# The first attention of an attention and GELU kernel: a shift added in PSUM, a new order of its steps, and two small loads that change queues

## The chip, the cores and the metric

The kernel runs on one core of one Trainium2 chip. Its time is the device time of one execution in microseconds (us). All times inside an execution count from the start of the profiled span.

## What is computed

q and k ([8, 12, 448, 64]: batch, head, position, dimension) are normalised by their root mean square and scaled by a gain; then follow softmax attention with v, and two dense layers with a GELU between them. The reference, cut to that:

```python
def rmsnorm(x, g):
    rms = np.sqrt(np.mean(x * x, axis=-1, keepdims=True) + 1e-06)
    return x / rms * g
q_n, k_n = (rmsnorm(q, g_q), rmsnorm(k, g_k))
scores = q_n @ k_n.transpose(0, 1, 3, 2) / 8.0
attn = softmax(scores)                  # max taken off, exp, divided by the sum
x = (attn @ v).transpose(0, 2, 1, 3).reshape(3584, 768)
h = x @ w_in                            # 768 -> 2048
c = np.float32(np.sqrt(2.0 / np.pi))
g = 0.5 * h * (1.0 + np.tanh(c * (h + 0.044715 * h * h * h)))
return g @ w_out                        # 2048 -> 768
```

In place of each row's maximum the kernel takes one shift for all scores off the exponent, worked out from the gains: `shift = min(0, 60 - bound)`, where the bound comes from the largest product of the two gains (L824 to L837). It does not change the quotient.

## The kernel before

**Tiling.** A batch has three groups (c = 0, 1, 2) of four heads. In a group, q and k lie on 128 partitions as 2 heads x 64 rows, with two pairs of heads (a) and seven pieces (t) of 64 positions beside each other. A unit (L327) is the scores of one piece of k against all 448 positions of q, for four heads: four matmuls of 64x64 weights, which fill a PSUM tile `t` of 128 x 2 x 448. There are two such tiles in the first attention, taken in turn (`pair`, L70). `exp` (L338) is one ScalarE instruction per unit: exp(scale x scores + shift), 128x896, written in bf16. So a batch has 21 units and 21 exponentials.

**What a group needs before its units.** The raw loads; squares (`square`, L157) and their sums along a row (`total`, L170, on VectorE); `rsqrt` (L193): a Ln and one or two Exp on ScalarE that give 1/root-mean-square; `normed` (L271): raw times that root, in bf16; `turn` (L289): transposes on TensorE, 128x128 each, seven for q and seven for k, into a PSUM bank `tp`; `put` (L299): the copy out of it into `qT` and `kT`, on VectorE for most, where k is also multiplied by both gains. k is normed and turned in two parts, pieces 0 to 3 (`t_first`) and 4 to 6 (`t_rest`).

**What follows the units.** `products` (L369): the sums of the exponentials (weights `ones`) and their products with v, in packs of four matmuls; then on VectorE a transpose of the sums (`turned`, L391), the reciprocal, its spread over the partitions (`spread`, L402) and the multiplication into `xT` (`quad_x`, L416). The first layer (`mm1_pair`, L541) reads `xT` and `w_in`; the second reads `w_out` and is laid between the units of the next batch's attention (L488, the quartered matmuls).

**What sets the order.** The program is scheduled by hand: each engine does its instructions in the order in which the code issues them. The first attention (L700) goes through slots 0 to 20: the loads of `side`, one unit, its exponential, then the steps that `mid` (L852) lists for the slot. Ahead of it stand the loads, the norms of group 0 and the shift. Idle matmuls (`idle`, L266) fill TensorE there. The bank pool `ps_m` has two PSUM banks; the transposes, the roots of group 2 and the sums of groups 1 and 2 share them.

**Queues.** q and k are asked for by SyncE's queue (SP), except the second half of the very first q, which ScalarE's queue asks for, followed there by g_k. v, w_in and w_out go through GpSimd's queue (POOL), in POOL's program order, between the squares that POOL does.

Of the kernel before, what the change touches and what calls it, by code (L numbers as in the profile page):

```python
# [17 lines left out]
def kernel(  # L18
# [20 lines left out]
    R = 64  # L39
# [48 lines left out]
    def load_g(i, row, eng):  # L88
        eng.dma_start(
            grow[:, i].rearrange("(j p) d -> j p d", j=2)[:, 0],  # L90
            row.rearrange("(j d) -> j d", j=2),
        )
# [12 lines left out]
    shift = consts.tile([P, 1], F32)  # L105
    eps = consts.tile([P, 1], F32)
    win = wts.tile([128, HP, d_ff], BF16)
# [62 lines left out]
    def total(b, c, n, hs=both, ts=slice(0, NT)):  # L170
        if b not in sss:
            sss[b] = smp.tile([P, NCH, 2, 2, NT], F32, tag="ss", name="ss")
        nc.vector.reduce_sum(  # L173
            sss[b][:, seat(b, c), "qk".index(n), hs, ts], squares(b, c, n, hs, ts), axis=AX.X
        )
# [17 lines left out]
    def rsqrt(b, c=slice(0, NCH), ns=both, near=(), ts=slice(0, NT), twice=False):  # L193

        if b not in rinvs:
            rinvs[b] = smp.tile([P, NCH, 2, 2, NT], F32, tag="rinv", name="rinv")
        lg = smp.tile([P, NCH, 2, 2, NT], F32, tag="lg", name="lg")
        nc.scalar.activation(  # L198
            lg[:, c, ns, :, ts], sss[b][:, c, ns, :, ts], AF.Ln, scale=1.0 / D, bias=eps
        )  # L200
# [124 lines left out]
    exs, ess, oas, scs = {}, {}, {}, {}  # L325

    def unit(b, c, t):  # L327

        sc = scs[b, c, t] = pair("sc")
        for a in range(2):  # L330
            rs = slice(a * D, (a + 1) * D)
            for r in range(2):
                nc.tensor.matmul(  # L333
                    sc[r * R:(r + 1) * R, a, :S], kT[rs, c, t, r], qT[b][rs, c, :, r],
                    start=True, stop=True,
                )

    def exp(b, c, t):  # L338
        if (b, c) not in exs:
            exs[b, c] = exq.tile([P, NT, 2, S], BF16, tag="ex", name="ex")  # L340
        nc.scalar.activation(  # L341
            exs[b, c][:, t], scs.pop((b, c, t))[:, :, :S], AF.Exp, scale=scale, bias=shift
        )
# [383 lines left out]
    def plan(*entries):  # L727
        steps = {}
        for slot, *fns in entries:
# [7 lines left out]
    halves += [  # L737
        lambda ts=ts: nc.sync.dma_start(  # L738
            raws["k", 0, 0][:, :, ts].rearrange("p a t d -> p a (t d)"),
            k[0, :4].rearrange("(a r) (p t) d -> r p a t d", r=2, t=NT)[:, :, :, ts]  # L740
            .rearrange("r p a t d -> (r p) a (t d)"),
        )
        for ts in (t_first, t_rest)
    ]
# [7 lines left out]
    nc.vector.memset(eps, 1e-6)  # L752
    for i in range(3):
        nc.vector.memset(ones[:, i * D // 4:(i + 1 + i // 2) * D // 4], 1.0)
    for i in range(2):
        nc.vector.memset(rows[:, i * P // 2:(i + 1) * P // 2], (D ** 0.5) * (1 + 2.0 ** -7))

# [52 lines left out]
    normed(0, 0, "q", nc.gpsimd, t_first)  # L810
    normed(0, 0, "q", nc.vector, t_rest)
    normed(0, 0, "k", nc.vector, t_first)
    total(0, 0, "k", ts=t_rest)
    square(0, 1, "q", nc.gpsimd)
    for a in range(2):
        square(0, 1, "k", nc.gpsimd, slice(a, a + 1))
    load_v(0, 0, 2)
# [3 lines left out]
    w_in_part(0, 2)  # L821
    for j in range(2):
        rs = slice(j * 32, (j + 1) * 32)
        nc.tensor.matmul(gall[:, j, :32], rows[rs], gbf[rs], start=True, stop=True)  # L824
    for ts in (t_rest, t_first):
# [7 lines left out]
    put(0, 0, "k", slice(0, 1))  # L833
    nc.vector.tensor_reduce(
        shift, gall[:, :, :32], axis=AX.XY, op=ALU.max, apply_absolute_value=True, negate=True
    )
# [5 lines left out]
    for a in range(2):  # L842
        total(0, 1, "k", slice(a, a + 1))

# [7 lines left out]
    mid = [(0, lambda: idle(2, warm())),  # L852
           (1, lambda: turn_new(0, t_rest), lambda: idle(2, warm())),
           (2, lambda: rsqrt(0, 1, near=(0, 1)), lambda: idle(2, warm())),
           (3, lambda: put(0, 0, "k", t_rest), lambda: normed(0, 1, "q", nc.vector),
            lambda: normed(0, 1, "k", nc.vector, t_first), lambda: idle(2, warm())),
           (4, lambda: idle(2, warm())),
           (5, lambda: turn(0, 1, "q"), lambda: put(0, 1, "q"),
            lambda: turn_new(1, t_first), lambda: put(0, 1, "k", t_first)),
           (6, lambda: total(0, 2, "q"), lambda: total(0, 2, "k")),  # L860
           (7, lambda: products(0, 0, 0, 0, 3)),
# [9 lines left out]
           (9, lambda: turn(0, 1, "k", t_rest), lambda: put(0, 1, "k", t_rest),  # L871
            lambda: normed(0, 2, "k", nc.vector, t_first),
            lambda: normed(0, 2, "k", nc.vector, t_rest), lambda: recip()),
           (10, lambda: products(0, 0, 1, 0, 3)),

           (11, lambda: products(0, 0, 1, 3, 5), lambda: turn(0, 2, "k", t_first),
            lambda: put(0, 2, "k", t_first), lambda: spread(slice(0, 1))),
           (12, lambda: turn(0, 2, "q"), lambda: put(0, 2, "q")),
           (13, lambda: turn_new(2, t_rest), lambda: put(0, 2, "k", t_rest),
# [156 lines left out]
```

## Time and profile before

| | us |
|---|---|
| median of 3 runs | 392.43 |
| lowest and highest | 391.71, 393.4 |
| the profiled execution | 392.21 |
| its span | 390.4 |
| PE (TensorE) busy | 381.5 (98%) |
| ACT (ScalarE) busy | 278.7 (71%) |
| DVE (VectorE) busy | 238.0 (61%) |
| POOL (GpSimd) busy | 125.2 (32%) |

The granted TensorE clock was 1.00. In the rows, `start us, us, engine line op out<-in shape xcount [idle before <-who ended it]` stands for one instruction or a run of equal ones; PEld is TensorE's weight load, an engine with a q behind it is its sequencer, which issues transfers. A row of the chain of waits has start, duration and what the end waited for in that time. A row of the windows has the stretch, its length, the busy time of each engine with the count of its instructions, the granted clock, the share of the 16 transfer engines and GB/s. A row of the transfers ends with the time from issue to landing. Neighbouring instructions on ACT and DVE overlap by about 0.1 us in these rows, so a run of three is shorter than three times one.

### The profile page before, as it was taken

Reading aid. Unit: us, or ns where it says so; the run is one execution under the profiler, and the core shown is the slowest. Engines: PE = TensorE matmul, PEld = TensorE weight load, DVE = VectorE, ACT = ScalarE, POOL = GpSimd, SP = SyncE. Lnnn points to the kernel's source line nnn. Section 1 sums busy time; section 2 is a strip of 40 time slices with the busy share of each in tenths; the row PEclk is TensorE's granted clock in tenths of the full one; section 3 lists DMA queues with packets and bytes.
Section 4 is the critical chain, followed back from the end, with each engine's and each line's share of the span. In section 5 each row is a group of like instructions: output and inputs, shape, how many; then the busy total and the mean of one; then the engine's idle time right before and its main releaser. Section 6 shows DMA issues by size and latency. Waiting matters only on the chain.

```text
span 390.4 us, 17468 instructions
## 1 busy us (share of the span) xinstructions
PE 381.5 (98%) x8023; PEld 290.2 (74%) x8023; DVE 238.0 (61%) x367; ACT 278.7 (71%) x353; POOL 125.2 (32%) x107
## 2 busy tenths in 40 slices
PE   8799999999999999999999999999999999999996
PEld 3365567777888788877888778877888778887664
DVE  5899938976597258835689256963598304980010
ACT  6895589767994689747996589946897449944300
POOL 4996504485004540083302740064400900000000
PEclk9999999999999999999999999999999999999999
DMA  8999999999713993359932996159622831220033
GB/s 272 311 212 210 210 169 330 210 210 240 150 44 87 230 217 73 80 104 234 194 78 65 157 273 113 44 111 249 107 64 64 123 44 35 52 65 4 2 81 82
DMA packets 64414, 54.68 MB, mean 140 GB/s; under 512 B 37588, under 2 KB 59988, under 8 KB 64340
## 3 DMA queue, kind: packets, MB, share of 16 engines
q1 hardware_dynamic: 53904, 41.33, 45.7%
q0 software_dynamic: 10128, 11.80, 18.5%
q8 instruction: 63, 1.03, 1.1%
q10 hardware_dynamic: 308, 0.43, 0.3%
q14 instruction: 11, 0.09, 0.1%
HBM read 45.61 MB, written 11.01 MB: 145 GB/s over the span
## 4 chain that ended last, share of the span: by engine, by line
PE 92%; ACT 4%; DMA 2%; POOL 1%; SPq 0%; DVE 0%; issue 0%; DVEq 0%
PE t L530 33%; PE t L488 32%; PE t L385 9%; PE t L333 7%; PE t L461 5%; PE t L549 4%; ACT ex L341 4%; DMA rawq<-in_q_dram 2%; POOL g L164 1%; PE h L434 1%; PE tp L294 0%; PE o L385 0%; SPq L738 0%; PE os L385 0%; DVE ss L173 0%; ACT lg L198 0%
## 5 line engine op out<-in xcount | busy, mean ns | idle before, releaser
L341 ACT ACTIVATE ex<-t,shift 128x896 bf16<-128x896 f32 x168 | 156.1, 1013 | 1.8 <-PE t L333 1.6
L488 PE MATMUL t<-wout,g 64*64 64x384 bf16 (+1 forms) x3456 | 151.5, 305 | 0.0
L530 PE MATMUL t<-xT,win 64*64 64x448 bf16 x2688 | 128.6, 349 | 0.0
L488 PEld LDWEIGHTS <-g 64*64 64x64 bf16 x3456 | 112.7, 107 | 20.6 <-issue 0.6
L530 PEld LDWEIGHTS <-win 64*64 64x64 bf16 x2688 | 96.4, 107 | 30.8
L536 ACT ACTIVATE g<-t 128x896 bf16<-128x896 f32 x56 | 50.5, 914 | 57.2 <-PE t L530 57.2
L173 DVE TENSOR_REDUCE ss<-sq 128x14 f32<-128x896 f32 (+3 forms) x45 | 44.6, 997 | 52.8 <-ACT sq L162 48.9
L333 PE MATMUL t<-qT,kT 64*64 64x448 bf16 x672 | 58.6, 351 | 3.1 <-ACT lg L198 1.6
L353 DVE TENSOR_TENSOR es<-ex 128x1792 bf16<-128x1792 bf16 x20 | 21.2, 1058 | 32.1 <-ACT ex L341 32.1
L276 POOL TENSOR_TENSOR nrmq<-rawq,rinv 128x896 bf16<-128x896 f32 (+1 forms) x21 | 34.7, 1652 | 16.5 <-ACT rinv L205 9.9
L786 POOL COPY mark<-es 1x1 bf16<-1x1 bf16 x6 | 1.1, 176 | 116.8 <-DVE es L360 112.6
L276 POOL TENSOR_TENSOR nrmk<-rawk,rinv 128x896 bf16<-128x896 f32 x20 | 33.7, 1686 | 0.0
L333 PEld LDWEIGHTS <-kT 64*64 64x64 bf16 x672 | 25.4, 106 | 10.4 <-DVE kT L303 3.6
L385 PE MATMUL t<-ex,vb 64*64 64x448 bf16 x588 | 32.1, 350 | 0.0
L395 DVE STREAM_TRANSPOSE st<-t 128x448 f32<-128x448 f32 x42 | 24.8, 627 | 9.3 <-PE t L385 9.3
L385 PEld LDWEIGHTS <-vb 64*64 64x64 bf16 x672 | 23.6, 107 | 7.0 <-issue 0.8
L407 DVE STREAM_TRANSPOSE rb<-rc 128x896 f32<-128x896 f32 (+1 forms) x25 | 26.7, 1067 | 0.3
L694 DVE COPY osb<-t 128x384 f32<-128x384 f32 (+1 forms) x4 | 2.0, 508 | 35.2 <-PE t L461 35.2
L420 DVE TENSOR_TENSOR xT<-t,rb 128x896 bf16<-128x896 f32 x21 | 22.8, 1087 | 0.8
L164 POOL TENSOR_TENSOR sq<-rawq 128x896 f32<-128x896 f32 (+1 forms) x9 | 13.6, 1515 | 28.3 <-DVE ss L173 21.6
L506 ACT COPY osb<-t 128x768 f32<-128x768 f32 (+1 forms) x18 | 12.6, 701 | 14.0 <-PE t L488 14.0
L356 DVE TENSOR_TENSOR es<-es,ex 128x1792 bf16<-128x1792 bf16 x20 | 21.3, 1063 | 0.8 <-ACT ex L341 0.8
(103 smaller groups left out, 313.6 us busy)
## 6 DMA issues: line engine op xcount, KB each, us to landing
rawq<-in_q_dram SPq DMA_DIRECT2D x23, 448.0 KB, 5.1
rawk<-in_k_dram SPq DMA_DIRECT2D x23, 448.0 KB, 6.0
out_dram<-osb SPq DMA_DIRECT2D x42, 192.0 KB, 2.7
vb<-in_v_dram POOLq DMA_DIRECT2D x6, 672.0 KB, 7.0
win<-in_moe_w_in_dram POOLq DMA_DIRECT2D x8, 384.0 KB, 11.1
wout<-in_moe_w_out_dram POOLq DMA_DIRECT2D x3, 768.0 KB, 18.4
out_dram<-osb SPq DMA_DIRECT2D x24, 96.0 KB, 3.1
vb<-in_v_dram POOLq DMA_DIRECT2D x2, 448.0 KB, 15.4
```

Source lines behind the costliest of these rows:

```text
L173: nc.vector.reduce_sum(sss[b][:, seat(b, c), "qk".index(n), hs, ts], squares(b, c, n, hs, ts), axis=AX.X)
L276: eng.tensor_mul(nrms[n, b, c][:, ts].rearrange("p t a d -> p a t d"), raws[n, b, c][:, :, ts], root[:, :, ts].to_broadcast([P, 2, m, D]),)
L333: nc.tensor.matmul(sc[r * R:(r + 1) * R, a, :S], kT[rs, c, t, r], qT[b][rs, c, :, r], start=True, stop=True,)
L341: nc.scalar.activation(exs[b, c][:, t], scs.pop((b, c, t))[:, :, :S], AF.Exp, scale=scale, bias=shift)
L356: nc.vector.tensor_add(es, es, ex[:, 4:6])
L385: nc.tensor.matmul(o[r][a * D:(a + 1) * D], vb[b % 2][rs, 2 * c + a, i] if what else ones[rs], es[i][rs, a], start=(i == 0), stop=(i == n ...
L395: nc.vector.transpose(st[:, r].rearrange("p a b -> p (a b)"), o[r])
L407: nc.vector.transpose(oas["rb"][:, rs].rearrange("p r s -> p (r s)"), rc.to_broadcast([128, (rs.stop - rs.start) * m, 32]),)
L420: nc.vector.tensor_mul(xT[b][:, 2 * c:2 * c + 2], oas["o", c, 1][:, :, :S], oas["rb"])
L488: mm = nc.tensor.matmul(o[a * R:(a + 1) * R, bank, :hi - lo], g[rs, f, at:at + R], wout[rs, f, lo:hi], start=(turn == 0 and f == 0), stop= ...
L530: mm = nc.tensor.matmul(h[a * R:(a + 1) * R, j, :S], win[rs, c, at:at + R], xT[b][rs, c], start=begin and c == cs[0], stop=end and c == cs ...
L536: nc.scalar.activation(g[:, 2 * i:2 * i + 2, (b % 2) * S:(b % 2 + 1) * S], h[:, :, :S], AF.Gelu_apprx_tanh,)
```

## The change

It touches the start and the first attention alone.

1. For units 2 to 13 the shift is added to the scores in PSUM: four more matmuls ahead of the unit's own, with weights `shifts` (the shift in bf16, 64 columns) and a moving tile `eighth` of 0.125, which open the accumulation that the scores close. The exponential of these units has the constant 0 as its bias. The others still read the tile `shift`. The Ln of every `rsqrt` has a constant 1e-6 as bias, not the tile `eps`.
2. The second half of the square of k of group 1 moves from POOL to ScalarE, behind exponential 1, and its sum to that slot.
3. `mid` is written anew: the copy of the rest of k of group 0 moves from slot 3 to 2, the transposes and copies of group 1 from slot 5 to 6, the norm of the rest of k of group 2 from slot 9 to 12, the reciprocal and the first half of its spread from 9 and 11 to 12. Ten idle matmuls become six.
4. The shift is worked out earlier on DVE; the rest of the first k is asked for by ScalarE's queue, and g_k by SyncE's behind the first k.

```diff
+    def in_psum(b, c, t):
+        return b == 0 and 2 <= c * NT + t < 2 * NT
+
     def unit(b, c, t):
         sc = scs[b, c, t] = pair("sc")
-        for a in range(2):
+        parts = [(a, r) for a in range(2) for r in range(2)]
+        begun = in_psum(b, c, t)
+        if begun:
+            for a, r in parts:
+                rs = slice(a * D, (a + 1) * D)
+                nc.tensor.matmul(
+                    sc[r * R:(r + 1) * R, a, :S], shifts[rs], eighth[rs], start=True, stop=False
+                )
...
-                    start=True, stop=True,
+                start=not begun, stop=True,
...
-            exs[b, c][:, t], scs.pop((b, c, t))[:, :, :S], AF.Exp, scale=scale, bias=shift
+            exs[b, c][:, t], scs.pop((b, c, t))[:, :, :S], AF.Exp, scale=scale,
+            bias=0.0 if in_psum(b, c, t) else shift
...
-            lg[:, c, ns, :, ts], sss[b][:, c, ns, :, ts], AF.Ln, scale=1.0 / D, bias=eps
+            lg[:, c, ns, :, ts], sss[b][:, c, ns, :, ts], AF.Ln, scale=1.0 / D, bias=1e-6
...
-        for ts in (t_first, t_rest)
+        for ts, eng in ((t_first, nc.sync), (t_rest, nc.scalar))
...
-    load_g(1, g_k, nc.scalar)
+    load_g(1, g_k, nc.sync)
...
-    nc.vector.tensor_scalar(shift, shift, 60.0, 0.0, op0=ALU.add, op1=ALU.min)
+    nc.vector.tensor_scalar(
+        shifts, shift.to_broadcast([P, R]), 60.0, 0.0, op0=ALU.add, op1=ALU.min
+    )
+    nc.vector.tensor_copy(shift, shifts[:, :1])
...
+           (1, lambda: square(0, 1, "k", nc.scalar, slice(1, 2)),
+            lambda: total(0, 1, "k", slice(1, 2)),
...
-           (5, lambda: turn(0, 1, "q"), lambda: put(0, 1, "q"),
+           (6, lambda: turn(0, 1, "q"), lambda: put(0, 1, "q"),
...
+           (12, lambda: turn(0, 2, "q"), lambda: put(0, 2, "q"),
+            lambda: normed(0, 2, "k", nc.vector, t_rest), lambda: recip(),
+            lambda: spread(slice(0, 1))),
```

ScalarE, from exponential 1 to exponential 4 (`ex` of a PSUM tile `t`; `lg` is the Ln of the sums of group 1, `o` its root). Before:

```order
L341 ACTIVATE ex<-t_100,shift 128x896
L341 ACTIVATE ex<-t_101,shift 128x896
L198 ACTIVATE lg<-ss,eps 128x28
L214 ACTIVATE o_127<-lg 128x28
L341 ACTIVATE ex<-t_100,shift 128x896
```

Now:

```order
L355 ACTIVATE ex<-t_100,shift 128x896
L163 ACTIVATE g<-rawk 128x448
L355 ACTIVATE ex<-t_101 128x896
L199 ACTIVATE lg<-ss 128x28
L215 ACTIVATE o_128<-lg 128x28
L355 ACTIVATE ex<-t_100 128x896
```

The square of half a k (`g<-rawk`) has come between exponentials 1 and 2, and the shift and eps are no operands any more.

TensorE, in front of the transposes of q of group 1 (`tp<-ident,nrmq`). Before, the four matmuls of unit 5, in the tile t_100, stand there:

```order
L269 MATMUL o_126<-const-bfloat16-1.0 128x448
L333 LDWEIGHTS kT
L333 MATMUL t_100<-qT,kT 64x448
...
L294 LDWEIGHTS nrmq
L294 MATMUL tp<-ident,nrmq 128x128
```

Now it is unit 6, in t_101, opened by four matmuls of the shift (the last of them is shown):

```order
L342 LDWEIGHTS shifts
L342 MATMUL t_101<-eighth,shifts 64x448
L347 LDWEIGHTS kT
L347 MATMUL t_101<-qT,kT 64x448
...
L295 LDWEIGHTS nrmq
L295 MATMUL tp<-ident,nrmq 128x128
```

The transposes have moved behind one more unit.

VectorE, from the norm of the first part of k of group 2 (512 elements) to the copy of the last part of its transposes (384 elements into `kT`). Before:

```order
L276 TENSOR_TENSOR nrmk<-rawk,root 128x2x4x64
L276 TENSOR_TENSOR nrmk<-rawk,root 128x2x3x64
L400 RECIPROCAL rc<-st 128x28
L303 TENSOR_SCALAR kT<-tp,gcols 128x512
L407 STREAM_TRANSPOSE rb<-rc 128x448
L307 COPY qT<-tp 128x896
L303 TENSOR_SCALAR kT<-tp,gcols 128x384
```

Now:

```order
L277 TENSOR_TENSOR nrmk<-rawk,root 128x2x4x64
L304 TENSOR_SCALAR kT<-tp,gcols 128x512
L308 COPY qT<-tp 128x896
L277 TENSOR_TENSOR nrmk<-rawk,root 128x2x3x64
L415 RECIPROCAL rc<-st 128x28
L422 STREAM_TRANSPOSE rb<-rc 128x448
L304 TENSOR_SCALAR kT<-tp,gcols 128x384
```

The second norm, the reciprocal and the half spread have moved behind both copies. On GpSimd one square of half a k is gone ahead of the loads of v and w_in; nothing else has changed place there.

More of the change, by code (lines that the diff above doesn't have):

```diff
@@ L105 @@
     shift = consts.tile([P, 1], F32)
-    eps = consts.tile([P, 1], F32)
+    shifts = consts.tile([P, R], BF16)
+    eighth = consts.tile([P, S], BF16)
     win = wts.tile([128, HP, d_ff], BF16)
@@ L750 @@
     loads(0, 2)
-    nc.vector.memset(eps, 1e-6)
+    nc.vector.memset(eighth, 0.125)
     for i in range(3):
@@ L811 @@
     normed(0, 0, "q", nc.vector, t_rest)
+    for j in range(2):
+        rs = slice(j * 32, (j + 1) * 32)
+        nc.tensor.matmul(gall[:, j, :32], rows[rs], gbf[rs], start=True, stop=True)
     normed(0, 0, "k", nc.vector, t_first)
+    nc.vector.tensor_reduce(
+        shift, gall[:, :, :32], axis=AX.XY, op=ALU.max, apply_absolute_value=True, negate=True
+    )
     total(0, 0, "k", ts=t_rest)
     square(0, 1, "q", nc.gpsimd)
-    for a in range(2):
-        square(0, 1, "k", nc.gpsimd, slice(a, a + 1))
+    square(0, 1, "k", nc.gpsimd, slice(0, 1))
     load_v(0, 0, 2)
@@ L841 @@
     total(0, 1, "q")
-    for a in range(2):
-        total(0, 1, "k", slice(a, a + 1))
+    total(0, 1, "k", slice(0, 1))
     side = [(1, lambda: loads(1, 0)),
@@ L850, in turn_new @@
         turn(0, c, "k", ts)
[L852 to L857, printed above, removed]
[L858 to L860 removed]
+    mid = [(0, lambda: idle(1, warm())),
+           (1, lambda: square(0, 1, "k", nc.scalar, slice(1, 2)),
+            lambda: total(0, 1, "k", slice(1, 2)),
+            lambda: turn_new(0, t_rest), lambda: idle(1, warm())),
+           (2, lambda: rsqrt(0, 1, near=(0, 1)), lambda: put(0, 0, "k", t_rest),
+            lambda: idle(1, warm())),
+           (3, lambda: normed(0, 1, "q", nc.vector),
+            lambda: normed(0, 1, "k", nc.vector, t_first), lambda: idle(1, warm())),
+           (4, lambda: idle(1, warm())),
+           (5, lambda: idle(1, warm())),
+           (6, lambda: turn(0, 1, "q"), lambda: put(0, 1, "q"),
+            lambda: turn_new(1, t_first), lambda: put(0, 1, "k", t_first),
+            lambda: total(0, 2, "q"), lambda: total(0, 2, "k")),
            (7, lambda: products(0, 0, 0, 0, 3)),
```

22 lines of the change are left out of this document (7 added, 15 removed).

## The prediction

> **What bounds the kernel now.** I read the page's slices first: PE is nine tenths busy from start to end. Then the chain of waits, to see where PE does not set the pace itself.
>
> ```profile
> 2.18 6.81 DMA rawq<-in_q_dram
> 9.05 3.47 POOL g L164 x3
> 13.74 5.41 ACT ex L341 x6
> ...
> 31.54 3.13 PE t L549 x16
> ```
>
> The first 31 us hang on a load, three squares on POOL and then ACT's exponentials; from 31.5 us to the end all pieces of the chain are PE. So what moves the first layer's start (31.47, the first L549) is passed on to the end, unless something else holds PE behind it. Something does:
>
> ```profile
> 2.00:54.00 52.00, 47.56 (x509) 26.34 (x511) 42.37 (x88) 39.36 (x56) 34.02 (x37) 1.00 1.10 248
> 33.60 0.73 POOL L776 DMA_DIRECT2D wout<-in_moe_w_out_dram  x1
> wout<-in_moe_w_out_dram POOLq DMA_DIRECT2D x1, 384.0 KB, 20.7
> 54.35 0.14 PEld L488 LDWEIGHTS <-g 64*64 64x64 bf16 x7 [0.24 <-issue]
> ```
>
> The DMA share is 1.10 over 2 to 54 us: the transfer engines have no time left. The last piece of w_out, asked for at 33.60, lands 20.7 later, at 54.30, and PE goes on with the matmuls that read it at 54.35, after 0.24 us in which the weight loads stood still (I count 0.2 as wait). So the kernel before already arrives there a little too early. An earlier first layer would wait here for the same landing; a later one would not. **Gains are cut off at 54.3 us, losses are passed on**, less 0.2 us.
>
> **The change part by part.** I number the 21 units and exponentials of the first attention u0 to u20 and e0 to e20 and walk to three of them.
>
> *To e3: the wait of 1.45 us.*
>
> ```profile
> 3.88 1.04 ACT L162 ACTIVATE sq<-rawq 128x448 f32<-128x448 f32 x2 [0.27 <-DMA rawq<-in_q_dram]
> 8.95 2.80 ACT L341 ACTIVATE ex<-t,shift 128x896 bf16<-128x896 f32 x3
> 9.05 1.68 POOL L164 TENSOR_TENSOR g<-rawq 128x896 f32<-128x896 f32 x1 [1.66 <-DMA rawq<-in_q_dram]
> 10.69 1.82 POOL L164 TENSOR_TENSOR g<-rawk 128x448 f32<-128x448 f32 x2
> 10.76 1.61 DVE L173 TENSOR_REDUCE ss<-g 128x14 f32<-128x896 f32 x2 [1.26 <-POOL g L164]
> 12.54 0.62 DVE L173 TENSOR_REDUCE ss<-g 128x7 f32<-128x448 f32 x1 [0.17 <-POOL g L164]
> 13.20 0.32 ACT L198 ACTIVATE lg<-ss,eps 128x28 f32<-128x28 f32 x1 [1.45 <-DVE ss L173]
> 13.68 1.89 ACT L341 ACTIVATE ex<-t,shift 128x896 bf16<-128x896 f32 x2
> 36.28 1.73 ACT L556 ACTIVATE g<-t 128x896 bf16<-128x896 f32 x2 [4.35 <-PE t L549]
> ```
>
> The third square goes from POOL to ACT, behind e1. But POOL was not what held ACT for most of this wait: DVE's sum over q starts at 10.76, and the sums stand in line. The third one can start when the second is done, 10.76 + 1.61 less the 0.08 by which neighbours overlap, at 12.3 and not 12.54. Three exponentials take 2.80 and two such squares 1.04, so e1 ends near 10.9 and ACT's square near 11.4: it is hidden with 0.9 us to spare, and without that cover would cost its 0.5. The Ln loses its bias operand: the Exp of the same shape behind it takes 0.20, so the gain is between 0 and 0.13; I take 0.1. e3 starts at 13.68 - 0.25 - 0.1 = **13.33**. Of the 1.45 us, 0.9 stay, since nothing makes q land earlier.
>
> What an exponential with a constant bias takes is not in the trace. The Gelu of equal shape, from PSUM and without a bias operand, gives a pair in 1.73 where the pair of exponentials takes 1.89: 0.08 less each, pace 0.81 instead of 0.89. The bounds are 0 (one operand fewer can't cost more) and 0.08; I take 0.08 for e2 to e13, 1.0 us if ACT set the pace throughout. At 0, e4 would end 0.16 later and the forecast would rise by 0.2.
>
> *To e7: the transposes of the next q and k now stand behind u6, not u5.*
>
> ```profile
> 14.72 0.38 PE L333 MATMUL t<-qT,kT 64*64 64x448 bf16 x4 [0.31 <-ACT ex L341]
> 14.78 0.68 DVE L276 TENSOR_TENSOR nrmk<-rawk,o 128x512 bf16<-128x512 f32 x1
> 15.04 0.57 PE L294 MATMUL tp<-ident,nrmq 128*128 128x128 bf16 x7
> 15.64 0.62 DVE L307 COPY qT<-tp 128x896 bf16<-128x896 bf16 x1 [0.18 <-PE tp L294]
> 16.18 0.47 DVE L303 TENSOR_SCALAR kT<-tp,gcols 128x512 bf16<-128x512 bf16 x1
> 16.71 0.38 PE L333 MATMUL t<-qT,kT 64*64 64x448 bf16 x4 [0.48 <-DVE kT L303]
> 16.35 2.81 ACT L341 ACTIVATE ex<-t,shift 128x896 bf16<-128x896 f32 x3
> 16.93 0.74 PE L385 MATMUL o<-ex,ones 64*64 64x448 bf16 x12
> 17.68 0.93 PE L385 MATMUL o<-ex,ones 64*64 64x448 bf16 x16
> ```
>
> Scores go to two PSUM tiles in turn, so u(n) waits for the end of e(n-2); u5's row shows that wait. Before, u5 at 14.72 leads to transposes, two copies on DVE, u7 at 16.71 and its end at 17.09: 2.37 us, and e7 at 17.24 is not late. Now the same 2.37 us start from u6, which waits for e4. With e3 at 13.33 and a pace of 0.81 e4 ends at 15.06; the norms that the transposes read (14.78 + 0.68 before, 0.35 earlier now) are done by 15.1; u6 begins at 15.1 with its four shift matmuls (12 matmuls take 0.74, 16 take 0.93: 0.19 for each further four); the chain ends at 15.1 + 0.19 + 2.37 = 17.66, and **e7 starts near 17.70, 0.46 later than before**, with ACT idle for a whole us after e6. The lead of 0.35 has become a delay: the slot costs 0.8.
>
> *To e14: normed, reciprocal and spread of the third group moved from slots 9 and 11 to 12.*
>
> ```profile
> 19.13 1.17 DVE L395 STREAM_TRANSPOSE st<-o 128x448 f32<-128x448 f32 x2
> 20.36 0.76 PE L385 MATMUL o<-ex,vb 64*64 64x448 bf16 x10 [0.16 <-DVE st L395]
> 20.53 1.14 DVE L276 TENSOR_TENSOR nrmk<-rawk,root 128x512 bf16<-128x512 f32 x2
> 21.61 0.40 PE L294 MATMUL tp<-ident,nrmk 128*128 128x128 bf16 x4
> 22.05 0.48 DVE L303 TENSOR_SCALAR kT<-tp,gcols 128x512 bf16<-128x512 bf16 x1
> 22.45 0.63 DVE L407 STREAM_TRANSPOSE rb<-rc 128x448 f32<-128x448 f32 x1
> 22.26 0.56 PE L294 MATMUL tp<-ident,nrmq 128*128 128x128 bf16 x7
> 23.01 0.58 DVE L307 COPY qT<-tp 128x896 bf16<-128x896 bf16 x1
> 23.07 0.34 PE L294 MATMUL tp<-ident,nrmk 128*128 128x128 bf16 x3
> 23.74 0.36 PE L333 MATMUL t<-qT,kT 64*64 64x448 bf16 x4
> ```
>
> Before, both halves of the third k are normed by 21.67, so the last three transposes (23.07) wait for nothing and u14 follows at 23.74; e14, 0.43 behind that (0.36 and the handover), at 24.17. Now DVE's transposes of the sums end 0.46 later, at 20.77, and PE goes on at 20.82. The 1.25 us from 20.36 to 21.61 plus one shift group (0.19) put the first k transposes at 22.06, and their copy ends 0.92 later, at 22.98. The seven q transposes now write the bank that this copy reads (the other still holds the roots that the later norm wants); before, they started at 22.26 beside it. Now 23.04, with 0.57 + 0.04 + 0.58 the q copy ends at 24.23; then, and only then, the rest of k is normed (the smaller of the pair at 20.53, about 0.55 of 1.14): 24.7. The three transposes go at 24.75, u14 0.67 behind them as before, 25.42, and **e14 at 25.85, 1.68 later**. Reciprocal and spread, which filled DVE's wait before, now come behind.
>
> To the end of the attention: behind the norm DVE has the small reciprocal (0.3 by the gap between the pair's end at 21.67 and the copy at 22.05), half the spread (0.63) and only then the copy of the last k (under 0.48, what the larger one takes): it ends at about 25.9. The sums of the second group (PE, behind u14, at 25.6) take that copy's bank, so u15 and all behind it lose about 0.2 more. From e15 on ACT is gapless at the old pace. The first layer starts about 1.9 later, near 33.35.
>
> **Sum:** -0.35 + 0.81 + 1.22 + 0.2 = +1.9 at the first layer; less the 0.2 us wait for w_out, which a late PE does not have: **+1.7**. The profiled execution took 392.21 us (span 390.4, the rest around it); +1.7 gives **393.9**. The median shown is 392.43, 0.2 higher; I leave that in the range.
>
> *Edits costed at nothing.* The idle matmuls and the new shift tiles lie ahead of e3, inside the 0.9 us that stay; so does anything up to 0.9 us by which g_k comes late behind the first k (POOL's gain products need it, and through them the first q, e0 and ACT's square). POOL asks for v and w_in 0.9 earlier, one square's time; the transfer engines are full either way. ScalarE's queue gets 192 KB of the first k in place of g_k, and SyncE's the reverse:
>
> ```profile
> 1.20 1.10 ACTq L89 DMA_DIRECT2D grow<-in_g_k_dram  x1
> 4.00:5.00 1.00, 1.00 (x4) 0.44 (x3) 0.51 (x1) 1.00 (x3) 0.07 (x1) 1.00 0.91 240
> 7.00:8.00 1.00, 0.95 (x14) 0.70 (x14) 0.96 (x2) 0.91 (x3) 0.40 (x1) 1.00 1.02 369
> ```
>
> At 4 to 5 us, with the first k alone on one queue, the transfer engines were 0.91 busy, later with one queue 1.02: two queues could fill a hole of at most 0.3 us between 4 and 7 us. On SyncE's queue g_k stands where a load of k stood; if its issue takes 1.10 as on ACT's, the next q is asked for up to 0.6 later, while the queue still has the first k to move. I take 0 for both, with the next q 0.3 earlier and 0.6 later as ends; e3 and all behind it follow the next q's landing one for one. The Trainium skill ("DMA: Bandwidth & Descriptors", Issuing engines are not separate DMA queues) says that transfers issued by several engines run on the same 16 DMA engines and that only issue time is saved. By that rule the sum stays 393.9; by the row's bound it would be 393.6.
>
> **The rivals.**
> - *The next q lands over 1 us earlier.* Its 6.81 us from issue to landing are far more than 448 KB at 369 GB/s; if the split ends that, everything behind e3 moves with it: 1.3 earlier leaves +0.6 at the first layer, +0.4 in all, 392.7. Against it: the engines were full from 7 us on, and the same bytes go ahead of it. 0.15.
> - *ACT stays the bound* (the copies come in time after all): 0.35 at e3, 11 x 0.08 from e3 to e13 and 0.1 for the second Ln bring PE forward by 1.3. PE then waits for w_out at 54.3, and only a DMA queue that starts 0.9 us earlier on POOL could move that. Not slower: 392.2, down to 391.5 if half of it lands. Against it: e7's and e14's chains above. 0.15.
> - *The shift matmuls stand in line.* From u8 to u13 PE has four-packs and transposes in nearly every slot; if none of these six groups falls into a wait, 6 x 0.19 = 1.1 is added where I counted 0.3: 394.7, slower by 0.6%. It decides if PE shows no wait between u8 and u13. 0.20.
>
> **How the numbers follow.** The forecast has 0.50. 0.5% (1.96 us, about what a measurement of this kernel can tell from no change) ends at 394.4, near the forecast, so its upper part (0.15) counts as slower, with 0.17 of the last rival: slower 0.32. Faster by over 1.96 us needs the first attention and the w_out landing to come earlier together: 0.04. The rest, 0.64, is the same. The range 391.9 to 395.4 takes in the second rival and, on the other side, 0.7 beyond the third.
>
> **What would show it.** Right: a Ln before e3 that still waits about 0.9 us for DVE; ACT idle about 1 us before e7 and about 0.8 before e14, both released by PE; constant-bias exponentials near 0.92 us; the first L549-type matmul near 33.3; no wait at w_out's last piece. Wrong: e7 not late, or the next q landing before 8.5, or PE still waiting for w_out near 54 us.

## The result and the profile after

The changed kernel takes 395.25 us (median of 20 runs, 394.42 to 398.19) against 393.29 us of the kernel before (20 runs, 390.74 to 395.69): a ratio of 1.005, interval 1.0029 to 1.0072, so slower by 0.5%, clear of noise, and just at the 0.5% where the prediction drew its line between no change and slower. The forecast was 393.9, with a range of 391.9 to 395.4, so the time lies at the range's upper end. Of the 1.35 us that are missing, 0.86 is that the kernel before has its median at 393.29 and not at 392.43. Between the two profiled executions (394.46 and 392.21) the loss is 2.25 us, forecast 1.7. Five executions of the experiments below (1426 us in the second, 814 us in the third, and three of the kernel before at 397.1 to 397.3) lie so far above the others of their kernel that the ratios leave them out.

ScalarE's rows of the changed kernel, from the first exponential to the last (start, duration, what; in brackets the idle time before and who ended it):

```profile
9.61 1.91 ACT L355 ACTIVATE ex<-t,shift 128x896 bf16<-128x896 f32 x2 [0.52 <-DVE shift L854]
11.41 0.57 ACT L163 ACTIVATE g<-rawk 128x448 f32<-128x448 f32 x1
11.88 0.91 ACT L355 ACTIVATE ex<-t 128x896 bf16<-128x896 f32 x1
12.67 0.23 ACT L199 ACTIVATE lg<-ss 128x28 f32<-128x28 f32 x1
12.94 0.20 ACT L215 ACTIVATE o<-lg 128x28 f32<-128x28 f32 x1
13.07 3.32 ACT L355 ACTIVATE ex<-t 128x896 bf16<-128x896 f32 x4
17.44 1.86 ACT L355 ACTIVATE ex<-t 128x896 bf16<-128x896 f32 x2 [1.05 <-PE t L347]
...
22.01 0.92 ACT L355 ACTIVATE ex<-t 128x896 bf16<-128x896 f32 x1 [0.45 <-PE t L347]
23.23 0.92 ACT L355 ACTIVATE ex<-t 128x896 bf16<-128x896 f32 x1 [0.31 <-PE t L347]
24.36 0.92 ACT L355 ACTIVATE ex<-t 128x896 bf16<-128x896 f32 x1 [0.21 <-PE t L347]
26.07 1.01 ACT L355 ACTIVATE ex<-t,shift 128x896 bf16<-128x896 f32 x1 [0.79 <-PE t L347]
27.37 5.50 ACT L355 ACTIVATE ex<-t,shift 128x896 bf16<-128x896 f32 x6 [0.29 <-PE t L347]
```

e0 is 0.66 later than before (9.61, was 8.95), e3 0.61 earlier (13.07, was 13.68), and the wait of 1.45 before the Ln is gone; e7 is 0.20 later and e14 1.90. The brackets tell where: 1.05 before e7, 0.45, 0.31 and 0.21 before e11 to e13, and 0.79 before e14, each ended by PE.

The start holds what was not foreseen. These are the issue of the next q on SyncE, its line in the transfers (the last number is from issue to landing), GpSimd's squares and VectorE's shift:

```profile
2.37 0.38 SPq L125 DMA_DIRECT2D rawq<-in_q_dram  x1
```

```profile
rawq<-in_q_dram SPq DMA_DIRECT2D x1, 448.0 KB, 5.2
```

```profile
7.60 1.68 POOL L165 TENSOR_TENSOR g<-rawq 128x896 f32<-128x896 f32 x1
9.23 0.93 POOL L165 TENSOR_TENSOR g<-rawk 128x448 f32<-128x448 f32 x1
```

```profile
8.69 0.64 DVE L851 TENSOR_SCALAR shifts<-shift 128x64 bf16<-128x64 f32 x1
9.36 0.15 DVE L854 CAST shift<-shifts 128x1 f32<-128x1 bf16 x1
```

The next q landed at 7.5, not 8.98, and GpSimd squares it from 7.60, not from 9.05. VectorE's new 64-column shift takes 0.64 us for very little data and ends at 9.33, just behind GpSimd's square (9.28); e0 waits for the small copy behind it.

Behind e3, these are PE's and then VectorE's rows at the two moved places:

```profile
15.33 0.56 PE L295 MATMUL tp<-ident,nrmq 128*128 128x128 bf16 x7
17.00 0.38 PE L347 MATMUL t<-qT,kT 64*64 64x448 bf16 x4 [0.57 <-DVE kT L304]
...
24.99 0.34 PE L295 MATMUL tp<-ident,nrmk 128*128 128x128 bf16 x3 [0.68 <-DVE nrmk L277]
25.66 0.36 PE L347 MATMUL t<-qT,kT 64*64 64x448 bf16 x4
```

```profile
15.93 0.62 DVE L308 COPY qT<-tp 128x896 bf16<-128x896 bf16 x1 [1.08 <-PE tp L295]
16.47 0.47 DVE L304 TENSOR_SCALAR kT<-tp,gcols 128x512 bf16<-128x512 bf16 x1
...
22.72 0.48 DVE L304 TENSOR_SCALAR kT<-tp,gcols 128x512 bf16<-128x512 bf16 x1 [1.04 <-PE tp L295]
23.84 0.62 DVE L308 COPY qT<-tp 128x896 bf16<-128x896 bf16 x1 [0.64 <-PE tp L295]
24.39 0.54 DVE L277 TENSOR_TENSOR nrmk<-rawk,root 128x384 bf16<-128x384 f32 x1
```

Read the pairs crosswise: u7 (17.00) waits for VectorE's copies, which waited 1.08 for the transposes; the last transposes (24.99) wait for the norm at 24.39, which stands behind the q copy. The first layer starts at 33.62 (was 31.47), and PE no longer waits at w_out:

```profile
33.62 0.55 PE L564 MATMUL t<-xT,win 128*128 128x448 bf16 x2
```

### The profile page after: what moved, and what is told of

Its sections match the earlier page's. It is cut to its first block, busy times and chain, and to the rows that moved or that the text cites. A ratio compares the mean times of both kernels' runs of the same rounds, so it can differ in the third digit from the quotient of the medians.

```text
span 392.5 us, 17557 instructions
## 1 busy us (share of the span) xinstructions
PE 383.5 (98%) x8067; PEld 291.4 (74%) x8067; DVE 237.4 (60%) x368; ACT 277.7 (71%) x354; POOL 124.3 (32%) x106
## 4 chain that ended last, share of the span: by engine, by line
PE 93%; ACT 2%; DVE 2%; DMA 1%; issue 0%; SPq 0%; POOL 0%; DVEq 0%; ACTq 0%
PE t L545 32%; PE t L503 32%; PE t L400 9%; PE t L347 8%; PE t L476 5%; PE t L564 4%; ACT ex L355 2%; PE o L400 1%; DMA rawk<-in_k_dram 1%; PE tp L295 1%; PE h L449 1%; PE os L400 0%; DVE qT L308 0%; DVE kT L304 0%; DVE st L410 0%
## 5 line engine op out<-in xcount | busy, mean ns | idle before, releaser
L503 PE MATMUL t<-wout,g 64*64 64x384 bf16 (+1 forms) x3456 | 150.6, 305 | 0.0
L355 ACT ACTIVATE ex<-t,shift 128x896 bf16<-128x896 f32 x156 | 145.3, 1018 | 3.6 <-PE t L347 2.9
L503 PEld LDWEIGHTS <-g 64*64 64x64 bf16 x3456 | 112.6, 107 | 19.6 <-PE t L503 0.3
## 6 DMA issues: line engine op xcount, KB each, us to landing
win<-in_moe_w_in_dram POOLq DMA_DIRECT2D x8, 384.0 KB, 11.6
```

Source lines behind the costliest of these rows:

```text
L355: nc.scalar.activation(exs[b, c][:, t], scs.pop((b, c, t))[:, :, :S], AF.Exp, scale=scale, bias=0.0 if in_psum(b, c, t) else shift)
L503: mm = nc.tensor.matmul(o[a * R:(a + 1) * R, bank, :hi - lo], g[rs, f, at:at + R], wout[rs, f, lo:hi], start=(turn == 0 and f == 0), stop= ...
```

## The experiments

The theory is that the two moved places cost the time. Its rivals are the shift matmuls, the late start, and a landing of the next q that is chance or the work of the queues. All ratios are to the kernel before on the same chip. The places, from one profiled execution each (us):

| kernel | next q lands | e0 | e3 | e7 | e9 | e14 | first layer | ratio to before |
|---|---|---|---|---|---|---|---|---|
| before | 8.98 | 8.95 | 13.68 | 17.24 | 19.62 | 24.17 | 31.47 | 1 |
| changed | 7.53 | 9.61 | 13.07 | 17.44 | 19.67 | 26.07 | 33.62 | 1.005 |
| 1 slot 5 | 7.10 | 10.56 | 14.17 | 18.25 | 20.44 | 26.84 | 34.38 | 1.006 [1.0039, 1.0081] |
| 2 norm in 9 | 7.45 | 9.54 | 12.99 | 17.36 | 19.59 | 25.12 | 32.45 | 1.0037 [1.0012, 1.0061] |
| 3 both | 6.99 | 10.44 | 13.89 | 17.51 | 19.69 | 25.22 | 32.54 | 1.0015 [0.999, 1.0041] |
| 4 queues alone | 6.61 | 9.24 | 12.41 | 15.97 | 18.36 | 22.90 | 30.20 | 0.9969 [0.9941, 0.9997] |
| 5 old queues | 7.36 | 9.62 | 13.08 | 17.45 | 19.68 | 26.09 | 33.62 | 1.0043 [1.0022, 1.0064] |
| 6 no lock | 7.17 | 9.20 | 12.66 | 17.02 | 19.26 | 25.66 | 33.20 | 1.0033 [1.0018, 1.0048] |
| 7 fewer | 7.40 | 9.51 | 12.96 | 16.57 | 18.76 | 23.74 | 31.04 | 1.0012 [0.9988, 1.0035] |
| 8 all | 7.30 | 10.76 | 14.33 | 17.94 | 20.13 | 25.11 | 32.41 | 0.9966 [0.9938, 0.9993] |
| 9 before again | 8.15 | 8.96 | 12.86 | 16.41 | 18.80 | 23.34 | 30.65 | one execution |
| 10 before, third | 9.41 | 8.99 | 14.12 | 18.31 | 20.82 | 25.61 | 32.91 | one execution |
| 11 square on GpSimd | 7.31 | 10.08 | 13.59 | 17.20 | 19.38 | 24.37 | 31.67 | 0.9967 [0.9942, 0.9991] |
| 12 old queues again | 8.45 | 8.98 | 12.79 | 17.16 | 19.40 | 25.80 | 33.34 | one execution |

Since e0 moves by up to 1.8 us from row to row, the steps behind it are read as differences within a row.

### 1 to 3: the two places

The first experiment moves the transposes and copies of group 1 back, the second the norm, reciprocal and spread of group 2, the third both:

```diff
-           (5, lambda: idle(1, warm())),
-           (6, lambda: turn(0, 1, "q"), lambda: put(0, 1, "q"),
-            lambda: turn_new(1, t_first), lambda: put(0, 1, "k", t_first),
-            lambda: total(0, 2, "q"), lambda: total(0, 2, "k")),
+           (5, lambda: turn(0, 1, "q"), lambda: put(0, 1, "q"),
+            lambda: turn_new(1, t_first), lambda: put(0, 1, "k", t_first)),
+           (6, lambda: total(0, 2, "q"), lambda: total(0, 2, "k")),
```

```diff
-            lambda: normed(0, 2, "k", nc.vector, t_first)),
+            lambda: normed(0, 2, "k", nc.vector, t_first),
+            lambda: normed(0, 2, "k", nc.vector, t_rest), lambda: recip()),
...
-            lambda: put(0, 2, "k", t_first)),
-           (12, lambda: turn(0, 2, "q"), lambda: put(0, 2, "q"),
-            lambda: normed(0, 2, "k", nc.vector, t_rest), lambda: recip(),
-            lambda: spread(slice(0, 1))),
+            lambda: put(0, 2, "k", t_first), lambda: spread(slice(0, 1))),
+           (12, lambda: turn(0, 2, "q"), lambda: put(0, 2, "q")),
```

> The changed kernel with the transposes and copies of group 1 back in slot 5 (one idle matmul of that slot goes). Theory A (the new places of the transposes and of the norm cost the time): in the changed kernel ACT stood 1.05 us before e7; that falls below 0.4, e7 starts near 16.7 instead of 17.44, the first layer near 32.9 instead of 33.62, and the whole takes about 0.7 us less than the changed kernel, 1.003 of the kernel before. Rival B (the shift matmuls, the shift's new operation and the late start cost it): e7 moves by less than 0.3 us, or what it gains is gone by e14, and the ratio stays at 1.005.

> The changed kernel with the norm of the rest of k of group 2 and the reciprocal back in slot 9, half the spread back in slot 11. Theory A: ACT's wait of 0.79 us before e14 falls below 0.3, e14 starts near 24.9 instead of 26.07, the first layer near 32.4 instead of 33.62: 1.2 us less than the changed kernel, 1.002 of the kernel before. Rival B: DVE only does the same work sooner and makes PE's first k transposes of group 2 late instead; e14 stays after 25.6 and the ratio at 1.005.

> The changed kernel with both places as before; it keeps the shift in PSUM, the square on ACT, the early shift and the new queues. Theory A: e3 at 13.1 as in the changed kernel, e7 near 16.7, e14 near 23.8, the first layer near 31.0 to 31.5, so 0 to 0.5 us before that of the kernel before and 2.2 to 2.6 ahead of the changed kernel; ratio 0.998 to 1.000, PE without a wait of over 0.2 at the last piece of w_out. Rival B: first layer at 32.5 or later, ratio at least 1.003.

From e3 to e7 the changed kernel takes 4.37, the second 4.37, the third 3.62: the slot of the transposes costs **0.75**. From e9 to e14 they take 6.40, 5.53 and 5.53: the norm's place costs **0.87**, and the wait before e14 is gone. So theory A holds for both places. It misses on the whole time: the third still starts the first layer at 32.54, not 31.5, because e0 came at 10.44 and because e9 to e14 is not back at the 4.55 of before. The first even gained nothing: from e3 to e7 it takes 4.08, not 3.62. Its row of e0 and its windows (start and end, length, busy time of PE, PEld, DVE, ACT and POOL, granted clock, DMA share, GB/s) show a second price of the late e0:

```profile
10.56 1.90 ACT L355 ACTIVATE ex<-t,shift 128x896 bf16<-128x896 f32 x2 [1.47 <-DVE shift L854]
```

```profile
9.00:11.00 2.00, 0.66 (x9) 0.21 (x5) 1.97 (x4) 0.53 (x2) 2.00 (x4) 1.00 1.06 387
11.00:12.00 1.00, 0.92 (x12) 0.41 (x12) 1.00 (x2) 1.00 (x2) 1.00 (x2) 0.84 1.05 378
12.00:13.00 1.00, 1.00 (x9) 0.10 (x1) 0.81 (x3) 1.00 (x3) 1.00 (x1) 0.50 1.08 379
```

The wait before e0 has grown to 1.47, PE is idle for two thirds of 9 to 11 us, and behind that its granted clock is 0.50 up to 15.1 us. The third, with as late an e0, kept 1.00. The rivals were not altogether wrong: something else costs time too, at the start and behind e9.

### 4: the queues alone

The kernel before with the queues changed, and nothing else.

```diff
-        lambda ts=ts: nc.sync.dma_start(
+        lambda ts=ts, eng=eng: eng.dma_start(
...
-        for ts in (t_first, t_rest)
+        for ts, eng in ((t_first, nc.sync), (t_rest, nc.scalar))
...
-    load_g(1, g_k, nc.scalar)
+    load_g(1, g_k, nc.sync)
```

> The kernel before with the two queues alone changed (rest of the first k asked for by ScalarE, g_k by SyncE behind the first k). Theory A (the split itself moves the landing): the next q lands near 7.5 as in the changed kernel, not 8.98; the first k or g_k lands 0.7 to 0.8 later, so the first square of k and e0 come 0.4 to 0.7 later; POOL's square of q starts about 1.0 earlier, the wait of 1.45 before e3 falls under 0.6 and e3 comes 0.3 to 0.7 earlier; at the end at most 0.4 less, ratio 0.998 to 1.000, since w_out's last piece holds PE. Rival B (the earlier landing is an accident of one execution, or comes from other parts of the change): the next q lands at 8.5 or later, nothing moves.

The next q landed at 6.61, e0 came 0.29 later and e3 1.27 earlier, and the first layer begins at 30.20. Theory A holds, but for one thing: the gain was to be cut off at w_out. SyncE's line of the next q, GpSimd's issues of w_out's last two pieces, and the last piece's line in the transfers:

```profile
rawq<-in_q_dram SPq DMA_DIRECT2D x1, 448.0 KB, 4.2
```

```profile
31.63 1.42 POOL L776 DMA_DIRECT2D wout<-in_moe_w_out_dram  x2
```

```profile
wout<-in_moe_w_out_dram POOLq DMA_DIRECT2D x1, 384.0 KB, 19.2
```

The last piece is asked for at 32.33 (half of the 1.42 behind 31.63) and lands 19.2 later, at 51.5 and not 54.3. Of these 2.8 us, 1.27 are the earlier issue and the rest the shorter transfer. The landing moved forward with the start, and PE did not wait for it. Still the profiled execution is no shorter than that of the kernel before (span 390.9 and 390.4): PE stood still for 1.05 us at 58 us and for 0.73 at 70 us, and the trace names nothing that it waited for. The ratio of 0.9969 is 1.2 us of 393, with an interval that goes from 0.1 to 2.3.

### 5, 6 and 12: the wide shift operation

The fifth is the changed kernel with the old queues, and the twelfth is the same kernel profiled once more:

```diff
-        for ts, eng in ((t_first, nc.sync), (t_rest, nc.scalar))
+        for ts, eng in ((t_first, nc.sync), (t_rest, nc.sync))
...
-    load_g(1, g_k, nc.sync)
+    load_g(1, g_k, nc.scalar)
```

The sixth keeps the new queues, but lets the wide operation read PSUM:

```diff
+    summed = gall[:, 1, S + 2 * NT:S + 2 * NT + 1]
     nc.vector.tensor_reduce(
-        shift, gall[:, :, :32], axis=AX.XY, op=ALU.max, apply_absolute_value=True, negate=True
+        summed, gall[:, :, :32], axis=AX.XY, op=ALU.max, apply_absolute_value=True, negate=True
     )
...
-        shifts, shift.to_broadcast([P, R]), 60.0, 0.0, op0=ALU.add, op1=ALU.min
+        shifts, summed.to_broadcast([P, R]), 60.0, 0.0, op0=ALU.add, op1=ALU.min
```

> The changed kernel with the queues of the kernel before (both parts of the first k on SyncE's, g_k on ScalarE's). Theory A (the wide shift operation on DVE, 128x64 from SBUF, can't run beside a GpSimd operation and waits for its end; the early landing of the next q is what puts GpSimd's square over it): the next q lands near 9.0, GpSimd's square of q starts at 9.0, after the shift operation, which takes about 0.2 us instead of 0.64; e0 starts near 9.0 instead of 9.61; e3 near 13.2 to 13.4, since the sums now wait for the late squares. Rival B (the operation is slow by its 64 columns): it takes 0.5 us or more here too. The whole time: 1.003 to 1.006 of the kernel before, since the places behind e6 stay.

> The changed kernel with the reduced shift written to PSUM, so that the wide shift operation reads PSUM and not SBUF. Theory A: it takes about 0.2 us although GpSimd's square runs beside it; e0 starts near 9.2 instead of 9.61, e3 near 12.65 instead of 13.07, the first layer near 33.2 instead of 33.62; ratio 1.003 to 1.005. Rival B: it takes 0.5 us or more, e0 stays at 9.5 or later.

> The changed kernel with the old queues, a second look (the same kernel as in the fifth experiment). So far the next q landed at 8.98, 8.15 and 9.41 in three looks at the kernel before, at 6.6 to 7.5 in all looks with the new queues, and at 7.36 in the one look with the old queues under the changed kernel. Theory A (the old queues let one late part through, more or less of it by chance): here it lands anywhere from 7.3 to 9.4, most likely above 7.6. Rival B (it is something else in the changed kernel that ends the late part): it lands at 7.0 to 7.5 again.

The same operation and GpSimd's square of q, in the fifth, the twelfth and the sixth:

```profile
8.56 0.77 DVE L851 TENSOR_SCALAR shifts<-shift 128x64 bf16<-128x64 f32 x1
```

```profile
7.61 1.68 POOL L165 TENSOR_TENSOR g<-rawq 128x896 f32<-128x896 f32 x1
```

```profile
8.34 0.18 DVE L851 TENSOR_SCALAR shifts<-shift 128x64 bf16<-128x64 f32 x1
```

```profile
8.52 1.68 POOL L165 TENSOR_TENSOR g<-rawq 128x896 f32<-128x896 f32 x1 [1.09 <-DMA rawq<-in_q_dram]
```

```profile
8.56 0.21 DVE L852 TENSOR_SCALAR shifts<-t 128x64 bf16<-128x64 f32 x1
```

```profile
7.61 1.67 POOL L165 TENSOR_TENSOR g<-rawq 128x896 f32<-128x896 f32 x1
```

The fifth and the twelfth are one kernel: 0.77 us where GpSimd is in its square, ending at 9.33 as the square ends at 9.29, and 0.18 where GpSimd still waits for its q. From PSUM it takes 0.21 beside the square. In the first experiment it lost to the second square as well: 1.66 us, to 10.28, when that ended at 10.22. So the operation waits for GpSimd; its 64 columns are not what it costs. The sixth gains just this: e0 9.20, and every later place 0.41 to 0.42 earlier, ratio 1.0033.

The Trainium skill ("SBUF — State Buffer", Who interferes with whom) says that VectorE and GpSimd share one pair of SBUF ports as an exclusive lock, which a tensor_scalar between SBUF operands can need, and that the loser blocks for the whole instruction. These runs agree: 0.18 alone, 0.64 to 1.66 against GpSimd.

On the queues the fifth spoke against my expectation: with the old ones the next q landed at 7.36, and everything down to the first layer (33.62) is as in the changed kernel. The twelfth, the same kernel, has it at 8.45, so one execution settles nothing here. Over all of them the old queues give 8.98, 8.15, 9.41, 7.36 and 8.45, the new ones 6.61 to 7.53 in nine: about 1.3 us earlier on the mean. Which of the two loads that change queues does it was not tried. There is a price at the other end: the first part of the first k lands at 5.07 to 6.02 with the new queues and at 4.65 to 4.81 with the old. And in the changed kernel the earlier q is worth little. If q lands late, the sums wait; if it lands early, the shift does. First layer 33.34 in the twelfth, 33.62 in the changed kernel.

### 7 and 8: fewer units in PSUM, and all together

The third experiment's places, with the shift in PSUM for units 2 to 8 alone; the eighth has the sixth's edit too.

```diff
-        return b == 0 and 2 <= c * NT + t < 2 * NT
+        return b == 0 and 2 <= c * NT + t < 9
```

> The kernel with both places as before (third experiment), and the shift in PSUM for units 2 to 8 alone; 9 to 13 have it as bias again. Theory A (from u9 on PE sets the pace, so the five groups of shift matmuls stand in line): the waits of ACT before e11 (0.44) and e12 (0.31) fall below 0.1, e14 comes about 5.1 to 5.2 behind e9 (20.51 to 24.17 is 4.55 from e9's 19.62 before; 5.53 in the third experiment), so 0.4 to 0.9 earlier. Rival B (DVE's copies and norms set the pace there): e14 stays 5.4 or more behind e9. The start may again lose 0.6 to 1.6 at the wide shift operation, so it is e9 to e14 that counts; ratio 0.998 to 1.002.

> Both places as before, the shift in PSUM for units 2 to 8 alone, and the wide shift operation reading PSUM: what remains of the change is the square on ACT, constant biases for seven units, the early shift and the queues. Theory A: e0 near 9.2, e3 near 12.5, e7 near 16.2, e14 near 23.3, the first layer near 30.6 against 31.47 of the kernel before and 33.62 of the changed one; ratio 0.996 to 0.999. If gains stop at the landing of w_out's last piece, PE waits there and the ratio is not under 0.998; if that landing comes forward with the rest (51.5 where the queues alone were changed), PE does not wait and the ratio is near 0.997. Rival B: the shift matmuls and the square on ACT cost as much as they save, first layer later than 31.2.

PE behind e9 in the changed kernel, without any idle time between the rows:

```profile
20.43 1.17 PE L400 MATMUL o<-ex,vb 64*64 64x448 bf16 x12
21.25 0.54 PE L342 MATMUL t<-eighth,shifts 64*64 64x448 bf16 x4
21.44 0.54 PE L347 MATMUL t<-qT,kT 64*64 64x448 bf16 x4
21.63 0.72 PE L400 MATMUL o<-ex,vb 64*64 64x448 bf16 x8
```

ACT from e9 on in the seventh:

```profile
18.76 1.89 ACT L355 ACTIVATE ex<-t,shift 128x896 bf16<-128x896 f32 x2
20.91 9.30 ACT L355 ACTIVATE ex<-t,shift 128x896 bf16<-128x896 f32 x10 [0.26 <-PE t L347]
```

e9 to e14 takes 4.98 instead of 5.53, though each exponential is 0.09 longer: the shift matmuls of units 9 to 13 stand in line there and cost **0.55** net. A wait of 0.26 before e11 remains, where less than 0.1 was expected. Counted from e7 to e14, the kernel before takes 6.93, the seventh 7.17, the third 7.71 and the changed kernel 8.63. The eighth's median is 391.57 us, ratio 0.9966: it beats both kernels. Its place in the table misses the expectation because its profiled execution (393.99) is the slowest of its 12. The first k landed at 6.02 in it, and PE, with nothing to do for 2.15 us, lost its clock for the next 3.4 us:

```profile
8.09 0.19 PE L829 MATMUL t<-gbf,rows 32*128 32x32 bf16 x2 [2.15 <-DVE nrmq L277]
```

```profile
8.00:9.00 1.00, 0.91 (x8) 0.63 (x9) 1.00 (x4) 0.54 (x2) 1.00 (x2) 0.60 1.05 403
```

```profile
9.00:11.00 2.00, 2.00 (x13) 0.82 (x11) 1.41 (x6) 1.34 (x5) 2.00 (x2) 0.50 1.05 387
```

### 9 and 10: the kernel before, profiled again

> The kernel before, unchanged, looked at once more. In its first profile the last of 16 parts of the next q landed at 8.98, 2.4 us behind the middle one (6.62); with the old queues under the changed kernel it landed at 7.36. Theory A (the late part is an accident of that one execution): here it lands at 7.0 to 8.0, GpSimd's square of q starts at 7.5 to 8.0, ACT's wait of 1.45 before the Ln is under 0.7, e3 starts near 12.5 and the first layer near 30.3 instead of 31.47, unless PE stalls elsewhere. Rival B (the old queues in the kernel before do it): it lands at 8.5 or later again and the first layer begins at 31.2 or later.

> The kernel before, unchanged, a third look, for the spread: theory A, the next q at 7.0 to 8.0 and the first layer near 30.3; rival B, 8.5 or later and 31.2 or later.

GpSimd's square of q, whose wait ends with the landing, in the two:

```profile
8.22 1.68 POOL L164 TENSOR_TENSOR g<-rawq 128x896 f32<-128x896 f32 x1 [0.81 <-DMA rawq<-in_q_dram]
```

```profile
9.48 1.68 POOL L164 TENSOR_TENSOR g<-rawq 128x896 f32<-128x896 f32 x1 [2.05 <-DMA rawq<-in_q_dram]
```

Neither theory holds as I put it: the landing moves by 1.3 us from one execution to the next, and e3 with it (12.86 and 14.12), yet it stays later than with any new queue. The first layer moves by 2.26 (30.65 and 32.91); the other 1.0 lies between e3 and e14 of the tenth, where PE's granted clock was 0.50 from 15.4 to 18.9 us, after 12 to 14 us almost without work. 31.47 is near the middle. Both executions lost time further on, at a place where the trace names nothing:

```profile
58.98 1.00 PE L488 MATMUL t<-wout,g 64*64 64x384 bf16 x18 [1.55 <-issue]
```

```profile
62.33 1.00 PE L488 MATMUL t<-wout,g 64*64 64x384 bf16 x18 [2.63 <-issue]
```

### 11: the square back on GpSimd

The eighth experiment's kernel with both halves of the square of k on GpSimd.

```diff
-    square(0, 1, "k", nc.gpsimd, slice(0, 1))
+    for a in range(2):
+        square(0, 1, "k", nc.gpsimd, slice(a, a + 1))
...
-           (1, lambda: square(0, 1, "k", nc.scalar, slice(1, 2)),
-            lambda: total(0, 1, "k", slice(1, 2)),
+           (1, lambda: total(0, 1, "k", slice(1, 2)),
```

> The eighth experiment's kernel with both halves of the square of k of group 1 on GpSimd, as before: what remains of the change is constant biases and PSUM shift for units 2 to 8, the early shift (reading PSUM) and the queues. Theory A (with the next q landing near 7.4 ACT has no wait left to hide the square, so it costs its 0.46): from e0 to e3 it takes 3.1 to 3.2 us instead of 3.57, and the first layer starts 21.0 to 21.3 behind e0 instead of 21.65; ratio 0.994 to 0.998. Rival B (GpSimd is late without the help, as it was before): DVE's third sum waits for GpSimd, e0 to e3 takes 3.5 or more, ratio 0.997 or higher.

Inconclusive. e0 to e3 took 3.51, not 3.1 to 3.2, but this execution too ran at half clock, from 8.3 to 11.7 us, and e2 waited 0.30 for PE. The ratio, 0.9967 against 0.9966, shows no price of the square. In the fourth, with the square on GpSimd and pointer biases, e0 to e3 takes 3.17; in the changed kernel e2 starts 1.36 behind e1 where it was 0.89, so 0.47 of the path is the square.

## Why the prediction was right or wrong

**e3 (13.33, came at 13.07): nearly the right size, by a wrong path.** The step that failed is "Of the 1.45 us, 0.9 stay, since nothing makes q land earlier". q landed 1.45 earlier, before the 8.5 that the prediction names as a sign of being wrong, and the wait before the Ln was gone. By its own terms, too, 0.8 and not 0.9 would have stayed (1.45 less 0.25, less the 0.5 of the square, with the 0.08 by which e2 is shorter). The earlier q alone would have given the first rival's gain, had the start not come later. Of e0's 0.66, 0.41 is the wide shift operation's wait for GpSimd (sixth experiment), which the prediction costed at nothing as "inside the 0.9 us that stay"; the other 0.25 stands beside the first k's square, which starts at 5.35 instead of 4.83; in the fourth, with the queues alone, e0 is 0.29 late. And with the cover gone the square on ACT costs the 0.5 that the prediction named for that case. So two edits that look apart work against each other: the earlier q puts GpSimd's square over VectorE's operation.

**e7: right.** From e3 to e7 4.37 was forecast and 4.37 measured, with ACT idle for 1.05 (forecast 1.0). Undone, it gives 0.75 back, of 0.8 claimed.

**e14: the wait right, its price in part another's.** From e7 to e14 8.15 was forecast and 8.63 measured; the wait before e14 was 0.79 (forecast 0.8). The missing 0.48 has two parts. One is a slip in the sum: behind 20.82, "1.25 us from 20.36 to 21.61 plus one shift group (0.19)" end at 22.26 and not at 22.06; the group was named and not added. With it e14 comes at 26.05 (measured 26.07) and the sum is +1.9, 394.1. The other is 0.27 between e7 and the end of VectorE's transposes of the sums (17.70 to 20.77 forecast, 17.44 to 20.78 measured). There unit 8's shift matmuls stand in front of the products, PE has no wait from 17.00 on, and VectorE waits for it:

```profile
17.79 0.36 PE L342 MATMUL t<-eighth,shifts 64*64 64x448 bf16 x4
19.14 0.55 DVE L277 TENSOR_TENSOR nrmk<-rawk,o 128x384 bf16<-128x384 f32 x1 [0.21 <-PE o L400]
```

Both are the rival "the shift matmuls stand in line", which thus came true in part. And the prediction put the whole 1.22 that it forecast from e7 to e14 on the norm's place. Undone, that place gives back 0.87; the seventh experiment puts 0.54 on the shift matmuls of units 9 to 13, and 0.24 is left over the kernel before (together 1.65 of the 1.70 by which the way from e7 to e14 grew). Shift matmuls of units 2 to 8 alone were not taken out, so that this 0.24 is theirs is argued, not shown.

**To the first layer: right.** 7.50 forecast behind e14, 7.55 measured. **Losses passed on: right.** 2.15 at the first layer, 2.1 in the span; no wait at w_out's last piece. **Gains cut off at 54.3: wrong as a rule.** The landing is no fixed point. GpSimd reaches that issue by a chain of its own work that starts with the root of group 2, just ahead of e9: in 13 of the 14 executions it asks 13.95 to 14.01 behind e9 (33.60 behind 19.62 before, 32.33 behind 18.36 in the fourth). An earlier attention so asks earlier, w_out came at 51.5, and the gain of the fourth was not stopped there. In the changed kernel e9 came at 19.67, so the piece was asked for at 33.62, as before, while the first layer came 2.15 later.

**Constant bias: right.** 0.91 to 0.92 long, 0.80 apart (13.07 to e6 at 15.46), 0.81 forecast. **The queues: sized too small.** The row's bound was 0.3 earlier; the mean over the executions is about 1.3. The middle part of the load did come 0.2 earlier (6.43, was 6.62); the rest is the last part, which lags less. The Trainium skill's rule ("DMA: Bandwidth & Descriptors", Issuing engines are not separate DMA queues), by which only issue time is saved, is not borne out by these landings: the next q was asked for 0.2 later and landed earlier. The first rival, at 0.15, had its condition come true and its price not.

So the sum of +1.7 was right in sign by its mechanisms and near in size by luck as well: the 0.48 left out behind e7 met an e3 that was 0.26 earlier than forecast, for a reason that the forecast had ruled out. The rest of the distance to 395.25 is where the kernel before has its median.

## To carry to other kernels

Look for what an edit wakes on another engine: a load that comes earlier moves a GpSimd instruction, and that can hold a VectorE operation of 0.2 us for 1.7. Profile a start that hangs on transfers more than once before an argument is built on one landing; between three executions of the kernel before the first layer moved by 2.3 us, more than the whole change costs. An addition moved to TensorE is free only in the slots in which TensorE waits; the rows with an idle bracket say which these are.

## What the runs showed of the hardware

- A VectorE tensor_scalar of 128x64 from SBUF takes 0.18 us alone and 0.64 to 1.66 us against GpSimd's squares; from PSUM 0.21 beside them.
- After 2.15 us without work (5.94 to 8.09) TensorE's granted clock fell from 1.00 to 0.50, for 3.4 us (8.2 to 11.6, eighth experiment). After 9 to 11 us with 0.66 us of work it fell in the first experiment, and with 0.72 in the third it did not.
- The last of the 16 parts of a load lands up to 2.6 us behind the middle one (9.41 and 6.83 in the tenth).
- PE stood still for 1.05 to 2.63 us at L488 near 58 to 62 us, with no releaser, in three of the four executions profiled in the old order (fourth, ninth, tenth), and in none of the ten in the new one, where a wait of this kind is 0.2 to 0.4 us, at L503 near 285 to 288 us, in four. After the 2.63 us of the tenth the clock was 0.50 from 63.2 to 66.6 us. I did not find why PE stops. It may be part of why the kernel before spreads from 390.5 to 398.0 us; that is argued, not shown.
